# Projecting the last segment inside attention unit 0, with new step patterns for the other units

## The chip, the cores and the metric

The kernel runs on one core of a Trainium2 chip. The metric is the device time of one execution in microseconds, and lower is better. The time before is 1859.91 us, the median of three runs (1858.72, 1859.91 and 1860.71). A difference of about 0.2% (3.7 us) is the least that a measurement of this kernel can tell from no change.

## The reference

One transformer block on 2048 tokens of width 576 is computed in float32: adaptive layer norm, an attention with 32 heads of width 18 that works on four segments of 512 tokens and carries a memory from one segment to the next, its output projection, a second layer norm, and a gated feed-forward part with 4608 hidden columns.

```python
h = _layernorm(x) * (1 + ca) + sa
q, k, v = h @ wq, h @ wk, h @ wv            # 32 heads of 18 columns, N = 4 segments of L = 512 tokens
for s in range(N):
    logits = qs @ ks.T * scale + mask       # mask inside the segment
    a_dot  = softmax(logits) @ vs
    a_mem  = (phi(qs) @ M) / (phi(qs) @ z + 1e-6)
    o      = g * a_mem + (1 - g) * a_dot
    M, z   = M + phi(ks).T @ vs, z + phi(ks).sum(0)
x = x + ga * (o @ wo)
h = _layernorm(x) * (1 + cb) + sb
x = x + gb * ((silu(h @ w_gate) * (h @ w_up)) @ w_down)
```

phi(t) is t + 1 where t is positive and exp(t) elsewhere. ca, sa, ga and the rest come from one small product, silu(c) @ w_mod.

## The kernel before

Matrix products keep float32 accuracy by splitting each operand into a rounded high part and a low part, so one product takes three passes. A **projection tile** is 128 of the 1152 columns of k and q for one segment: 14 matmuls of 512 columns into one PSUM bank (the PSUM buffer `pp`, line 100), then two ScalarE copies out of it (`fh` rounded, `f` full, lines 513 and 514), a VectorE subtraction (`fl`, line 515), and stores to DRAM on SyncE's queue (`kD`, `qD`, and for the q columns phi(q) in `qF`, lines 519 to 532). A segment has nine tiles; tiles 0 to 4 hold k, 4 to 8 hold q.

**Phase 1** runs a loop over the four segments. For each it does the nine tiles (`proj`), for segments 0 to 2 also the v projection (`vproj`) and the memory (`mem`), and it prepares the next segment: `load_x`, the layer norm, and `trans_in` (transposes, `pt`, line 255), which leaves the activations as `hh`, `hl` and `hr`. Between these pieces stand two side jobs in small steps: `early` (scores for the row maxima of units 0 and 1) and `late_mod` (the remaining columns of w_mod; its last result is `gbB`, PSUM `pc`, line 371). In phase 1 a scheduler sets the order of instructions on each engine. Its SBUF pools are released at its end, the weights `wqkh` and `wqkl` among them.

**Phase 2** opens its own pools (`sk2`, `vp`, `wk2`, `op2` and others, and PSUM `ps2`) and walks over 33 **units**; units 0 to 31 are four heads of one segment each, eight units to a segment. In phase 2 the order of instructions is the order of the code. Unit u has 12 **score steps** (`a` in the patterns). A step does the score matmuls of one bank for unit u's exponentials (`p2_step`, line 656, then ScalarE's exponential, line 662) and those of one bank for unit u+2's row maxima (`p1_step`, line 184, then VectorE's masked maximum, line 199). The matmuls of the two kinds sit on different halves of the array's rows and are issued in turn. Three banks serve each kind.

The other events of a unit are letters of a pattern, a row of eleven slots in `PAT`: `V` multiplies the previous unit's exponentials with v (line 679), `E` copies the result out of PSUM on ScalarE (line 691, `avs`), `c` and `d` transpose and normalize it, `m` transposes the row maxima of unit u+1 and `n` copies them out on ScalarE (line 218, `mr`) and sends them by two DMAs (line 173) into the stacked operand `qs`, from which unit u+1's scores read them. `M` and `X` are a quarter of an extra product and its way out: in units 0 to 7 the v projection of segment 3 (`v_m`, line 803), from unit 9 on the output projection (`wo_m`, line 784). `P`, `Q`, `q`, `Y` prepare wo; `f` and `h` load phi(q); `A`, `B`, `C`, `D`, `G` compute the memory part; `R`, `S`, `T`, `Z`, `z` transpose the attention output; `l`, `p`, `x` do the second layer norm. Rows 0 and 1 of `PAT` serve even and odd units in the first half of a segment, rows 2 and 3 in the second half. `KP` says at which slot further transposes of the later units are issued. All of the events that use the PSUM tag `x` share two banks.

At the start of unit u, `load_unit(u + 3)` puts four loads on SyncE's queue (line 168, `ks<-kD` and `qs<-qD`); the row maxima of that unit begin one unit later. Unit 0 in the kernel before uses row 0 of `PAT`; `V`, `E`, `m`, `c` and `d` do nothing in it.

After unit 32 come the rest of the output projection and the feed-forward part, in which nothing is changed.

Of the kernel before, what the change touches and what calls it, by code (L numbers as in the profile page):

```python
# [15 lines left out]
P = 128  # L16
# [28 lines left out]
PM = ()  # L45
KP = (10, 8, 10, 8)
WW = (11, 15, 18, 22, 27)
# [12 lines left out]
E2 = 2  # L60
PAT = (("a a", "a D G V0123 m", "n", "E a", "a Q a M0 M1", "M2 a a M3", "c q X Y P d", "a", "h a a Z R z S T", "a f", ""),
# [3 lines left out]
LNA = 1  # L65
# [9 lines left out]
def block(ctx: ExitStack, tc: tile.TileContext, x, wqk, wv, wo, beta, wgu, wd, c, w_mod, wm01, out):  # L75
# [12 lines left out]
    def run(g):  # L88
        for _ in g:
            pass  # L90

    def mm14(ps, wh, wl, xh, xl, xr):
        k = 0
        for kt in range(5):
            if kt < 4:
                pairs = [(wh(kt), xh(kt)), (wl(kt), xh(kt)), (wh(kt), xl(kt))]
            else:
                pairs = [(wh(4), xr()), (wl(4), xr())]
            for a, b in pairs:
                nc.tensor.matmul(ps, lhsT=a, rhs=b, start=(k == 0), stop=(k == 13))  # L100
                k += 1

# [162 lines left out]

    p2, p2r, p7 = ExitStack(), ExitStack(), ExitStack()
    yx2 = pool(p7, "yx2", side="right")
# [5 lines left out]
    def v_ops(s, i, h):  # L273
# [6 lines left out]
        return ops + [(hr[:, tk], wvh[:, 4, sl]), (hr[:, tk], wvl[:, 4, sl])]  # L280

    with ExitStack() as p1:
        wq1 = pool(p1, "wq1")
        raw = pool(p1, "raw1", 2)
# [26 lines left out]

        wqkh = wq1.tile([P, 9, 5, P], F32R, tag="wqkh", name="wqkh")
        wqkl = wq1.tile([P, 9, 5, P], F32R, tag="wqkl", name="wqkl")
        bdm = w1.tile([P, 5, 8, VW], F32, tag="bdm", name="bdm")
# [190 lines left out]
        def proj(s, t):  # L505
            hh, hl, hr = hT[s]
            pp = ps.tile([P, L], F32, tag="p", name="pp", bufs=3)
            mm14(pp, lambda k: wqkh[:, t, k, :], lambda k: wqkl[:, t, k, :], lambda k: hh[k],
                 lambda k: hl[k], lambda: hr)
# [6 lines left out]
            k0, k1 = 128 * t, min(128 * t + 128, D)  # L516
            if k0 < D:
                n = k1 - k0
                nc.sync.dma_start(kD[s][k0:k1, 0:2, :], f32(fh[:n]).unsqueeze(1).to_broadcast([n, 2, L]))
                nc.sync.dma_start(kD[s][k0:k1, 2, :], f32(fl[:n]))  # L520
            q0, q1 = max(128 * t - D, 0), 128 * t + 128 - D
            if q1 > 0:
                n = q1 - q0
                r = P - n
                nc.sync.dma_start(qD[s][q0:q1, 0:3:2, :], f32(fh[r:]).unsqueeze(1).to_broadcast([n, 2, L]))
                nc.sync.dma_start(qD[s][q0:q1, 1, :], f32(fl[r:]))
                if s > 0:
                    e = pb.tile([P, L], F32, tag="pq1", name="pq1")
                    nc.vector.tensor_scalar(e[r:], f[r:], 0.0, None, op0=ALU.min)
                    nc.scalar.activation(e[r:], e[r:], AF.Exp)  # L530
                    nc.vector.scalar_tensor_tensor(e[r:], f[r:], 0.0, e[r:], op0=ALU.max, op1=ALU.add)
                    nc.sync.dma_start(qF[s][q0:q1, :], e[r:])
            return f
# [36 lines left out]

        for s in range(NSEG):
            gens = []
            if s == 0:
                gens.append(load_wv())
            if s + 1 < NSEG:
                gens.append(prep(s + 1))
            g = chain(*gens)
# [6 lines left out]
            for t in QKORD:  # L584
# [16 lines left out]
                if s > 1 or s == 1 and t > 4:  # L601
                    next(gl, None)
            tg = trans_in(s + 1) if s + 1 < NSEG else iter(())
            for i in range(4):
                if i == 3:
                    for _ in g:
                        pass
                if s < 3:
                    vproj(s, i)
# [9 lines left out]
            if s < 3:  # L619
                for _ in mem(s):  # L620
                    next(tg, None)
            for _ in tg:
# [7 lines left out]
    wk = pool(p2, "wk2", 2)  # L630
    opl_ = pool(p2, "op2")
    ps = pool(p2, "ps2", 2, space=PSUM)
# [92 lines left out]

    w3 = pool(p2r, "w3", side="right")
    o3 = pool(p2r, "o3", 2, side="right")
    yt = {}

    def yh(k, kb):  # L730
        return yt[1][:, k - 1, kb] if k else yt[0][kb]

    woh = w3.tile([P, 5, D], F32R, tag="woh", name="woh")
    wol = w3.tile([P, 5, D], F32R, tag="wol", name="wol")

# [50 lines left out]
    def wo_x(s, i, h):  # L786
# [3 lines left out]
        if h == 1:  # L790
            (nc.scalar if (s, i) == (2, 3) else nc.sync).dma_start(xD[s][:, i, :], xr)

    vst3 = {}
# [114 lines left out]
    def event(ev, u):  # L908
        n, a = ev[0], ev[1:]
        s, q = divmod(u, 8)  # L910
        if n == "V":
            for j in a:
# [11 lines left out]
        elif n == "d":  # L924
            comb_b(u - 1)
        elif n == "f" and s < 3 and q < 4:
            phi_q(s + 1, q + 1)
        elif n == "h" and s < 3 and q == 0:
            phi_q(s + 1, 0)
# [17 lines left out]
        elif n in "MX":  # L947
            w = u - 9
            if u < 8:
                if n == "M":  # L950
# [484 lines left out]
    with tc.manual_schedule():  # L1435
        new_stack(3, sk2)
        load_unit(3)
        for j in range(4):
            load_v(0, j)
        ot[0] = opl_.tile([P, 4, D], F32, tag="o0", name="o0")  # L1440
        for u in range(NU + 1):
            s, q = divmod(u, 8)
            if u:
                load_unit(u + 3)
            ma, mb = [], []
# [290 lines left out]
```

## Time and profile before

| | |
|---|---|
| median of three runs | 1859.91 us |
| profiled execution: its time / its span | 1856.97 us / 1855.2 us |
| TensorE busy in the span | 1816.8 us (98%), granted clock 0.996 |
| VectorE / ScalarE / GpSimd busy | 1492.6 / 958.2 / 495.8 us |
| segment 3's tiles start in the trace at | 191.4 us |
| unit 0 / unit 1 start in the trace at | 223.0 / 238.6 us |
| unit 32's product with v starts at | 566.2 us |

How to read it: the profiled execution took 1.8 us more than its span, and 2.9 us less than the median. TensorE's busy time counts a matmul from its issue to its end, and these overlap, so 98% does not mean that no time is lost: where the order makes TensorE wait a little, its records only grow longer. What a stage costs is better read from where it starts and where the next one starts. All times below are microseconds from the start of the span.

### The profile page before, as it was taken

What the parts mean: (1) busy time and instruction counts of PE and PEld (TensorE: products, weight loads), DVE (VectorE), ACT (ScalarE), POOL (GpSimd) and SP (SyncE); (2) the same over time, 40 slices, a digit from 0 to 9 for tenths busy, and PEclk for the clock granted to TensorE, in tenths of its full rate; (3) what the DMA queues carried; (4) which work ended last, traced back from release to release, by engine and by line L of the source; (5) the groups of instructions that cost most, each with busy time, mean ns of one, the idle gap of its engine ahead of it and who ended that gap; (6) DMA issues with size and microseconds to landing.
All of it is one profiled execution on the core that took longest, in us unless ns stands there. A gap on an engine that the chain in (4) does not pass through costs nothing.

```text
span 1855.2 us, 31128 instructions
## 1 busy us (share of the span) xinstructions
PE 1816.8 (98%) x11061; PEld 1518.0 (82%) x11061; DVE 1492.6 (80%) x3309; ACT 958.2 (52%) x2137; POOL 495.8 (27%) x702
## 2 busy tenths in 40 slices
PE   8999989999999999999999999999999999999999
PEld 5888756666667888888888888888888888888888
DVE  7566468888886888888888888758888888888887
ACT  6344457667776545445445444434454544544441
POOL 2010036454563345545544544300000000000000
PEclk9999999999999999999999999999999999999999
DMA  8677565558658654555555444395332333334331
GB/s 298 224 242 253 212 175 154 152 149 217 177 149 278 218 185 157 172 194 176 166 183 168 132 137 167 125 297 172 127 105 85 120 105 107 100 102 127 104 100 52
DMA packets 178562, 304.49 MB, mean 164 GB/s; under 512 B 25304, under 2 KB 108184, under 8 KB 176616
## 3 DMA queue, kind: packets, MB, share of 16 engines
q1 hardware_dynamic: 151032, 248.66, 42.7%
q10 hardware_dynamic: 27376, 53.86, 8.2%
q8 instruction: 87, 1.43, 0.3%
q14 instruction: 67, 0.55, 0.1%
HBM read 188.42 MB, written 113.33 MB: 163 GB/s over the span
## 4 chain that ended last, share of the span: by engine, by line
PE 87%; DVE 6%; DMA 4%; issue 1%; ACT 1%; SPq 1%; POOL 0%; ACTq 0%; DVEq 0%; POOLq 0%
PE A L1273 24%; PE pd L1401 13%; PE C L1273 12%; PE pd L1382 10%; PE B L1273 6%; PE pp L100 5%; PE av L679 3%; PE pw L784 3%; PE pv L545 2%; DVE junk L199 2%; PE s L184 2%; PE s L656 2%; DMA qs<-qD 1%; PE pn L862 1%; DMA y<-yD 1%
## 5 line engine op out<-in xcount | busy, mean ns | idle before, releaser
L1273 PE MATMUL A<-y,wh 128*128 128x512 f32 x1152 | 406.1, 393 | 1.1 <-ACT B L1319 0.7
L199 DVE CUSTOM_DVE_ANT_0 junk<-s,tri 128x384 bf16<-128x384 f32 (+3 forms) x512 | 222.0, 486 | 45.8 <-PE s L184 27.2
L1238 DVE TENSOR_TENSOR wl<-O,wh 128x256 fp32r<-128x256 f32 x504 | 253.7, 509 | 2.1 <-ACT wh L1237 1.6
L1273 PEld LDWEIGHTS A<-y,wh 128*128 128x128 f32 x1152 | 216.6, 188 | 45.9 <-ACT B L1319 2.2
L1273 PE MATMUL A<-y,wl 128*128 128x512 f32 x576 | 226.8, 394 | 0.0
L1387 DVE TENSOR_TENSOR acc<-acc,pd 128x576 f32<-128x576 f32 x216 | 162.3, 752 | 59.4 <-PE pd L1382 51.5
L1273 PE MATMUL C<-y,wh 128*128 128x512 f32 x576 | 202.9, 393 | 1.1 <-DVE cu L1296 1.1
L662 ACT ACTIVATE Pt<-s 128x512 f32<-128x512 f32 (+2 forms) x384 | 179.1, 525 | 44.7 <-PE s L184 24.4
L1237 ACT CAST wh<-O 128x256 fp32r<-128x256 f32 x504 | 197.5, 405 | 1.7 <-DMA yD<-st 0.8
L1401 PE MATMUL pd<-dh,ah 128*128 128x288 f32 x640 | 188.9, 295 | 0.5 <-DVE x L1405 0.5
L1401 PE MATMUL pd<-dh,al 128*128 128x288 f32 x640 | 189.0, 295 | 0.0
L1401 PE MATMUL pd<-dl,ah 128*128 128x288 f32 x640 | 188.7, 295 | 0.0
L1411 DVE TENSOR_TENSOR acc<-acc,pd 128x576 f32<-128x576 f32 x156 | 117.0, 750 | 87.9 <-PE pd L1401 87.2
L1228 POOL TENSOR_TENSOR O<-O 128x384 f32<-128x384 f32 x132 | 149.6, 1148 | 135.3 <-DMA O<-in_wgu_dram 61.5
L1342 ACT CAST ah<-sg 128x512 fp32r<-128x512 f32 x192 | 119.1, 621 | 77.2 <-DVE sg L1297 70.3
L1343 DVE TENSOR_TENSOR al<-sg,ah 128x512 fp32r<-128x512 f32 x192 | 136.3, 710 | 10.0 <-ACT ah L1342 9.9
L1382 PE MATMUL pd<-dh,ah 128*128 128x288 f32 x448 | 133.0, 297 | 0.0
L1382 PE MATMUL pd<-dh,al 128*128 128x288 f32 x448 | 132.5, 296 | 0.0
L1382 PE MATMUL pd<-dl,ah 128*128 128x288 f32 x448 | 132.3, 295 | 0.0
L184 PE MATMUL s<-ks,qs 54*128 54x512 f32 (+1 forms) x480 | 122.9, 360 | 8.2 <-DVE mx L199 4.2
L656 PE MATMUL s<-qs,ks 56*128 56x256 f32 (+3 forms) x512 | 124.5, 356 | 3.4 <-ACT Pt L662 2.8
L1401 PEld LDWEIGHTS pd<-dh,ah 128*128 128x128 f32 x640 | 120.7, 189 | 6.8 <-DVE x L1405 0.8
(388 smaller groups left out, 4337.2 us busy)
## 6 DMA issues: line engine op xcount, KB each, us to landing
O<-in_wgu_dram SPq DMA_DIRECT2D x36, 768.0 KB
O<-oD SPq DMA_DIRECT2D x36, 512.0 KB
oD<-O ACTq DMA_DIRECT2D x34, 512.0 KB
ks<-kD SPq DMA_DIRECT2D x64, 216.0 KB
qs<-qD SPq DMA_DIRECT2D x64, 216.0 KB
O<-in_wgu_dram SPq DMA_DIRECT2D x36, 384.0 KB
rD<-wr ACTq DMA_DIRECT2D x36, 336.0 KB
wr<-rD SPq DMA_DIRECT2D x35, 336.0 KB
```

Source lines behind the costliest of these rows:

```text
L184: nc.tensor.matmul(bank[:, n * o:n * o + n], lhsT=qst[b][r, h // 2, 128 * i:128 * i + 128], rhs=kst[b][r, h // 2, 0:n], start=True, stop=True)
L199: nc.vector.tensor_tensor_reduce(junk[:, :n], bank[:, n * o:n * o + n], tri[:, L - n:], 1.0, -3e38, op0=ALU.add, op1=ALU.max, accum_out=mx ...
L656: nc.tensor.matmul(bank[:, n * o:n * o + n], lhsT=kst[u % NB][r, g // 2, 128 * j:128 * j + 128], rhs=qst[u % NB][r, g // 2, 128 * j:L], st ...
L662: nc.scalar.activation(pt[:, hs[0]:hs[-1] + 1:2, :n], bank[:, :n * per].rearrange("p (a b) -> p a b", a=per), AF.Exp, scale=SCALE)
L1228: eng.tensor_tensor(o[:, d], o[:, a], o[:, b], op=op)
L1237: nc.scalar.copy(wh, o)
L1238: later.append(lambda: nc.vector.tensor_tensor(wl, o, f32(wh), op=ALU.subtract))
L1273: nc.tensor.matmul(bank, lhsT=a, rhs=b, start=(first and n == 0), stop=(n == 6), skip_group_check=not first)
L1343: later.append(lambda: nc.vector.tensor_tensor(al, src, f32(ah), op=ALU.subtract))
L1382: nc.tensor.matmul(pd[:, i, :288], lhsT=a[:, tk], rhs=w, start=(k == 0), stop=(k == 2))
L1387: nc.vector.tensor_tensor(o, o, pd[:, :, :288], op=ALU.add)
L1401: nc.tensor.matmul(pd[:, i, :288], lhsT=a[:, tk], rhs=w, start=(k == 0), stop=(k == 5))
```

## The change

The loop of phase 1 runs over segments 0 to 2 only, still transposes segment 3's activations at its end, and takes `late_mod` in more steps during segment 2, so that it ends there. The weights of the k and q projections lie in a pool of their own (`p2q`) that stays open. The pools of phase 2 are opened next, and unit 3's operands are loaded. Unit 0 then has a pattern row of its own, the fifth. In it `Wt` is a quarter of segment 3's projection tile t (`seg3`; three or four matmuls, with the PSUM bank from the shared tag `x`), and `W9` a quarter of the v projection that unit 0 had before. What follows a tile's last matmul is done in the three quarters after it: the copies, the VectorE part, the exponential for phi(q), the stores. The tiles' SBUF buffers are two sets cut out of `pq` and `vq`, which are free until then. At unit 1 the weights' pool is closed, and the pools for wo and for the attention output are opened in its place. The first two `phi_q` loads move from unit 0 to unit 1. Rows 0 to 3 of `PAT`, and `KP`, have other entries; no event is added to or taken from a unit by this.

```diff
-KP = (10, 8, 10, 8)
+KP = (9, 7, 10, 9)
-PAT = (("a a", "a D G V0123 m", "n", "E a", "a Q a M0 M1", "M2 a a M3", "c q X Y P d", "a", "h a a Z R z S T", "a f", ""),
+PAT = (("a a Q D", "a G V0123 m E q", "", "a a", "a M0 M1", "n a a c Y M2 d M3 X", "", "a a", "h f a R P Z S T", "", "z a"),
...
+       ("W0 W0 W0 W0 a a a", "W1 W1 W1 W1 W2 W2 W2 W2 a a a", "W3 W3 W3 W3 W4 W4 W4 W4", "a a a", "W5 W5 W5 W5 W6 W6 W6 W6", "a a a", "W7 W7 W7 W7", "W8 W8 W8 W8", "W9 W9", "W9 W9", "P"))
...
-        for s in range(NSEG):
+        for s in range(3):
...
-                if t < 5 and s < 3:
+                if t < 5:
                     pend = (t, f)
...
+                if s > 1 and t < 5:
+                    next(gl, None)
...
+    def seg3(t):
+        if not tmp3:
+            a = sk2.tile([P, 5, L], F32, tag="pq", name="tmpa").rearrange("p a b -> p (a b)")
+            b = vp.tile([P, 4, VC], F32, tag="vq", name="tmpb").rearrange("p a b -> p (a b)")
+            for v in (a, b):
+                tmp3.append([v[:, L * i:L * i + L] for i in range(4)])
+        f, fh, fl, e = tmp3[t % 2]
+        fh, fl = fh.bitcast(F32R), fl.bitcast(F32R)
+        pp = ps.tile([P, L], F32, tag="x", name="pp", bufs=XB)
+        ops = p_ops(3, t)
+        for c in range(WC):
+            for n in range(14 * c // WC, 14 * (c + 1) // WC):
+                nc.tensor.matmul(pp, lhsT=ops[n][0], rhs=ops[n][1], start=(n == 0), stop=(n == 13))
+            if c < 3:
+                yield
+        nc.scalar.copy(fh, pp)
+        nc.scalar.copy(f, pp)
+        yield
+        _, q1, r = q_rows(t)
+        nc.vector.tensor_tensor(fl, f, f32(fh), op=ALU.subtract)
+        if q1 > 0:
+            nc.vector.tensor_scalar(e[r:], f[r:], 0.0, None, op0=ALU.min)
+        yield
+        if q1 > 0:
+            nc.scalar.activation(e[r:], e[r:], AF.Exp)
+            nc.vector.scalar_tensor_tensor(e[r:], f[r:], 0.0, e[r:], op0=ALU.max, op1=ALU.add)
+        yield
+        k_store(3, t, fh, fl)
+        q_store(3, t, fh, fl)
...
+            if u == 1:
+                while s3q:
+                    seg3_step(-1)
+                p2q.close()
...
-                for ev in PAT[q // 4 * 2 + u % 2][k].split():
+                for ev in PAT[q // 4 * 2 + u % 2 if u else 4][k].split():
...
+                elif u == 0 and 2 <= k < 6:
+                    load_v(0, k - 2)
```

The first place is TensorE between the last segment's projection and unit 0. `pp` is a projection tile, `s` a bank of scores. Before, the last tile of segment 3 ends and the score steps of unit 0 follow one on another:

```order
L100 MATMUL pp<-hl_2191,wqkh 128x512
L100 MATMUL pp<-hr,wqkh 128x512
L100 MATMUL pp<-hr,wqkl 128x512
L656 MATMUL s_2602<-qs_982,ks_983 128x512
L184 MATMUL s_2605<-ks_991,qs_990 128x512
L184 MATMUL s_2612<-ks_991,qs_990 128x512
L656 MATMUL s_2611<-qs_982,ks_983 128x512
L656 MATMUL s_2618<-qs_982,ks_983 128x512
L184 MATMUL s_2619<-ks_991,qs_990 128x512
L184 MATMUL s_2626<-ks_991,qs_990 128x512
L656 MATMUL s_2625<-qs_982,ks_983 128x512
L656 MATMUL s_2634<-qs_982,ks_983 128x384
```

Now they begin behind the first tile of segment 3, three steps at a time, and the next tile follows:

```order
L807 MATMUL pp<-hl_2197,wqkh 128x512
L807 MATMUL pp<-hr,wqkh 128x512
L807 MATMUL pp<-hr,wqkl 128x512
L661 MATMUL s_2369<-qs_982,ks_983 128x512
L174 MATMUL s_2372<-ks_991,qs_990 128x512
L174 MATMUL s_2379<-ks_991,qs_990 128x512
L661 MATMUL s_2378<-qs_982,ks_983 128x512
L661 MATMUL s_2385<-qs_982,ks_983 128x512
L174 MATMUL s_2386<-ks_991,qs_990 128x512
L807 MATMUL pp<-hh_2190,wqkh 128x512
L807 MATMUL pp<-hh_2190,wqkl 128x512
L807 MATMUL pp<-hl_2194,wqkh 128x512
```

All nine tiles stand so between four groups of three steps; in each tile the matmuls that read `hr` come last.

The second place is SyncE's queue at the same point. `ks_2588` and `qs_2587` are unit 3's operands, `ks_983` and `qs_982` unit 0's buffers, which unit 4 takes over. Before, unit 3's loads stand behind all of segment 3's stores:

```order
L525 DMA qD_90<-fh 128x2x512
L526 DMA qD_90<-fl 128x512
L532 DMA qF_98<-pq_2547 128x512
L125 DMA ks_2588<-ones 10x8x128
L125 DMA ks_2588<-ones 2x8x128
L168 DMA ks_2588<-kD_91 54x2x512
L168 DMA qs_2587<-qD_87 54x2x512
```

Now unit 3's loads stand ahead of the first of these stores, and behind the last of them come the loads for unit 4:

```order
L297 DMA qD_90<-tmpa 128x2x512
L298 DMA qD_90<-tmpa 128x512
L826 DMA qF_98<-tmpa 128x512
L1033 DMA woraw<-in_wo_dram 128x576
L158 DMA ks_983<-kD_91 54x2x512
L158 DMA qs_982<-qD_87 54x2x512
```

So what waits for the end of the last tile on this queue is no longer unit 3's load but unit 4's.

The third place is ScalarE in unit 2, an even unit in the first half of a segment (row 0). `Pt` is a score bank's exponential, `mr` the copy of the row maxima, `avs` the copy of the product with v. Before:

```order
L662 ACTIVATE Pt<-s_2937 128x512
L218 COPY mr<-pmt 32x128
L691 COPY avs<-av 128x512
L662 ACTIVATE Pt<-s_2970 128x512
L662 ACTIVATE Pt<-s_2979 128x384
L662 ACTIVATE Pt<-s_2986 128x384
L662 ACTIVATE Pt<-s_3007 128x384
```

Now:

```order
L667 ACTIVATE Pt<-s_2907 128x512
L696 COPY avs<-av 128x512
L667 ACTIVATE Pt<-s_2936 128x512
L667 ACTIVATE Pt<-s_2945 128x384
L667 ACTIVATE Pt<-s_2952 128x384
L208 COPY mr<-pmt 32x128
L667 ACTIVATE Pt<-s_2974 128x384
```

The copy of the row maxima has moved behind the copy of the product with v and behind three exponentials.

More of the change, by code (lines that the diff above doesn't have):

```diff
@@ L90, in run @@
             pass
[L92 to L101, printed above, removed]
     cst = pool(ctx, "cst")
@@ L505, in proj @@
         def proj(s, t):
-            hh, hl, hr = hT[s]
             pp = ps.tile([P, L], F32, tag="p", name="pp", bufs=3)
-            mm14(pp, lambda k: wqkh[:, t, k, :], lambda k: wqkl[:, t, k, :], lambda k: hh[k],
-                 lambda k: hl[k], lambda: hr)
+            for n, (a, b) in enumerate(p_ops(s, t)):
+                nc.tensor.matmul(pp, lhsT=a, rhs=b, start=(n == 0), stop=(n == 13))
             f = pb.tile([P, L], F32, tag="pf", name="pf")
@@ L515, in proj @@
             nc.vector.tensor_tensor(fl, f, f32(fh), op=ALU.subtract)
[L516 to L521, printed above, removed]
+            k_store(s, t, fh, fl)
+            q_store(s, t, fh, fl)
+            q0, q1, r = q_rows(t)
             if q1 > 0:
[L523 to L526, printed above, removed]
                 if s > 0:
@@ L618, in block @@
             next(tg, None)
-            if s < 3:
-                for _ in mem(s):
-                    next(tg, None)
+            for _ in mem(s):
+                next(tg, None)
             for _ in tg:
@@ L1444, in block @@
                 load_unit(u + 3)
+            if u == 1:
+                while s3q:
+                    seg3_step(-1)
+                p2q.close()
+                w3 = pool(p2r, "w3", side="right")
+                o3 = pool(p2r, "o3", 2, side="right")
+                opl_ = pool(p2, "op2", side="right")
+                woh = w3.tile([P, 5, D], F32R, tag="woh", name="woh")
+                wol = w3.tile([P, 5, D], F32R, tag="wol", name="wol")
+                ot[0] = opl_.tile([P, 4, D], F32, tag="o0", name="o0")
             ma, mb = [], []
```

80 lines of the change are left out of this document (59 added, 21 removed), and 6 rows, old and new, of the table PAT.

## The prediction

> **What bounds the kernel now.** I read the change first, and then only the stretch that it touches: from segment 3's first projection tile, at 191.4 us, to the end of the units, at about 570 us. The page says how long the profiled execution was, and the windows view cuts the start of that stretch into segment 3's tiles, unit 0, unit 1 and unit 2. Columns: stretch, length, then busy time and instructions of TensorE, weight loads, VectorE, ScalarE and GpSimd, then the granted TensorE clock, the DMA share and GB/s.
>
> ```profile
> span 1855.2 us, 31128 instructions
> ...
> 191.40:223.00 31.60, 31.60 (x143) 25.08 (x141) 11.91 (x21) 14.60 (x26) 1.43 (x2) 1.00 0.61 213
> 223.00:238.60 15.60, 9.89 (x48) 6.53 (x47) 8.74 (x36) 8.20 (x17) 3.72 (x10) 0.72 0.74 207
> 238.60:251.00 12.40, 12.10 (x86) 6.89 (x87) 6.88 (x31) 6.74 (x16) 3.49 (x7) 0.81 0.66 207
> 251.00:262.00 11.00, 9.99 (x89) 6.19 (x92) 9.72 (x42) 6.99 (x16) 4.33 (x11) 1.00 0.49 141
> ```
>
> The first row is TensorE alone: busy all of 31.6 us, with VectorE at 11.9 and ScalarE at 14.6. The second is the opposite: unit 0 takes 15.6 us with TensorE busy for 9.9, at a clock of 0.72, and the clock is still 0.81 in unit 1. The chain of waits says what holds it.
>
> ```profile
> 193.51 15.40 PE pp L100 x66
> ...
> 211.13 11.90 PE pp L100 x51
> ...
> 225.23 0.60 DVE junk L199
> 225.84 0.60 DVE junk L199
> ...
> 230.46 8.05 DMA qs<-qD
> ...
> 238.65 0.89 PE s L184 x2
> ...
> 285.00 8.04 DMA qs<-qD
> ```
>
> Tiles go at 15.40 / 66 = 0.233 us a matmul. Unit 0 then ends on unit 3's operands: their last load is issued at 230.46 and lands 8.05 us later, and unit 1's first scores start at 238.65. In the queue this load stands behind the stores of all nine tiles. So unit 0 costs 15.6 us for little TensorE work, because a load came late and nothing else was left to do.
>
> The units behind it are another regime. The product with v happens once a unit, so its rows are their beat:
>
> ```profile
> 239.77 4.14 PE L679 MATMUL av<-Pt,vq 128*32 128x512 f32 x32
> 251.62 2.36 PE L679 MATMUL av<-Pt,vq 128*32 128x512 f32 x32
> 261.94 2.36 PE L679 MATMUL av<-Pt,vq 128*32 128x512 f32 x32
> 271.99 2.36 PE L679 MATMUL av<-Pt,vq 128*32 128x512 f32 x32
> ...
> 559.27 2.36 PE L679 MATMUL av<-Pt,vq 128*32 128x512 f32 x32 [0.30 <-POOL Pt L666]
> ```
>
> From unit 2 to unit 31 are 29 units in 307.65 us, 10.61 each. The view of waits between 251 and 566 us gives what TensorE and its weight loads waited for around the scores (total, times, longest):
>
> ```profile
> PEld s L184 <- DVE mx L199: 11.2, 36, 1.0
> PEld s L656 <- ACT Pt L662: 7.6, 24, 0.9
> PE s L656 <- ACT Pt L662: 2.5, 8, 0.5
> PE s L184 <- DVE mx L199: 2.2, 5, 0.9
> ```
>
> That is 23.5 us in all, many small waits for a score bank, and this is what other step patterns can act on.
>
> **Term 1: unit 0 inside the tiles.** Before, the two first windows are 31.6 + 15.6 = 47.2 us. Now the same TensorE work stands in one run. The tiles and what stood between them stay at 31.6 us (gbB's two matmul pairs and the transposes move ahead of the tiles, and cost the same there). To it come unit 0's extra product and its twelve score steps, at full clock. The product is 14 matmuls of 288 columns; for the steps I take those of unit 10, from each group's first score to the next operation behind it:
>
> ```profile
> 570.16 2.07 PE pw L784 x14
> ...
> 337.72 0.50 PE L184 MATMUL s<-ks,qs 54*128 54x512 f32 x1
> ...
> 338.51 0.40 PE L784 MATMUL pw<-woh,hh 128*128 128x288 f32 x1
> ...
> 340.04 0.44 PE L656 MATMUL s<-qs,ks 56*128 56x384 f32 x1
> ...
> 340.58 0.40 PE L784 MATMUL pw<-wol,hh 128*128 128x288 f32 x1
> ...
> 341.75 0.38 PE L656 MATMUL s<-qs,ks 56*128 56x256 f32 x1
> ...
> 342.59 0.66 PE L758 MATMUL pto<-ident,o 128*128 128x128 f32 x4
> ```
>
> Three steps in 0.79 us, two in 0.54, three narrow ones in 0.84: 0.27 us a step, 3.3 us for twelve. With the product's 2.1 us this makes 31.6 + 3.3 + 2.1 = 37.0 us.
>
> One wait is added. Tile 0 now stands alone at the front and ends with `hr`, where before the scheduler mixed tiles 0 and 1.
>
> ```profile
> 192.42 0.78 ACT L262 ACTIVATE hh<-pt,colv 128x512 fp32r<-128x512 f32 x1 [2.90 <-PE pt L255]
> ...
> 195.23 0.69 DVE L264 TENSOR_TENSOR hr<-hf,hr 64x512 fp32r<-64x512 f32 x1 [0.63 <-ACT hf L263]
> ```
>
> `hr` was ready at 195.9, 4.5 us after the tiles began; tile 0's twelve matmuls ahead of it take 2.8. So up to 1.7 us is lost, and nothing if `hr` comes earlier by the 2.90 us that ScalarE sat idle for transposes, which now stand ahead of the last memory matmuls. I take 0.8, the middle. The stretch becomes 37.8 us, a gain of 47.2 - 37.8 = **9.4 us**.
>
> The other engines have room in it: ScalarE's 14.6 + 8.2 = 22.8 us and VectorE's 11.9 + 8.7 = 20.6 us fit under 37.8. Each score step puts about 0.6 us on both, three steps at once, and at least one tile (14 x 0.233 = 3.3 us) stands behind each group, so their banks come free under it.
>
> **Term 2: the clock.** Unit 1 took 251.62 - 239.77 = 11.85 us, unit 2 10.32 and unit 3 10.05; unit 1's product with v alone took 4.14 us instead of 2.36. Without the idle stretch before it I expect unit 1 to take what unit 2 took: **1.5 us** gained (0 if TensorE still idles enough, 1.8 by unit 3).
>
> **Term 3: what is late next.** The load that held unit 1 is now 40 us early. Behind the last store, though, stand the four loads for unit 4, which unit 2 needs. How long a last tile takes to its last store, and four such loads to be issued:
>
> ```profile
> 222.62 0.40 PE L100 MATMUL pp<-hr,wqkl 128*128 128x512 f32 x1
> ...
> 227.08 0.32 SPq L532 DMA_DIRECT2D qF<-pq  x1
> ...
> 229.22 0.42 SPq L168 DMA_DIRECT2D ks<-kD  x1
> ...
> 230.46 0.34 SPq L168 DMA_DIRECT2D qs<-qD  x1
> ```
>
> From the tile's end at 223.0 to its store's issue were 4.1 us, 2.9 without the two VectorE maxima of 0.60 that stood between. Unit 1 starts 2.1 us after the tile, behind the extra product. So the loads begin 0.8 to 2.0 us into unit 1, the last is issued 1.2 us later, and with 8.05 us it lands 10.1 to 11.3 us into a unit of 10.3. The wait is 0 to 1.0 us; I take **0.6 us** lost. The Trainium skill ("DMA: Bandwidth & Descriptors", section "Anatomy of one DMA") has about 2.0 us fixed and bytes over 436 GB/s: an estimate of 4 us for these 864 KB, no wait, and a sum 0.6 us better. The 8.05 and 8.04 us of the chain speak against it here, and I go by them.
>
> **Term 4: the patterns of units 1 to 31.** Each unit keeps its events. Row 1 had four score steps in a row with nothing of TensorE between them, for three banks; now there are three, and part of the extra product behind. In row 0 `c` and `d` now stand among score steps. No row of before prices this. Two units with row 0 or 1 and like work differ by 10.32 - 10.05 = 0.27 us; over 31 units that is 8.4 us, which I take as the end on both sides. Since the listed waits total 23.5 us and the one clear edit (row 1, eight units) goes against them, I take a tenth of them: **2.0 us** gained.
>
> **Sum.** 9.4 + 1.5 - 0.6 + 2.0 = 12.3 us. The profiled execution took 1856.97 us, so 1844.7 on its scale; it lies 2.9 us under the median, so I forecast 1859.91 - 12.3 = **1847.6 us**. With the ends of term 4 and the small ones the likeliest case spans 1840 to 1857.
>
> **Rivals.**
>
> *The row maxima arrive late (slower).* In row 0, ScalarE's copy `mr` now stands behind `avs` and three exponentials; behind it wait two DMAs on SyncE's queue, and the next unit's first score on TensorE.
>
> ```profile
> 337.83 0.26 ACT L218 COPY mr<-pmt 32x128 f32<-32x128 f32 x1 [1.77 <-PE pmt L214]
> 337.99 0.57 ACT L691 COPY avs<-av 128x512 f32<-128x512 f32 x1
> ...
> 338.47 1.33 ACT L662 ACTIVATE Pt<-s 128x512 f32<-128x512 f32 x3
> ...
> 338.11 1.29 SPq L173 DMA_DIRECT2D qs<-mr  x2
> ...
> 344.78 0.47 PE L656 MATMUL s<-qs,ks 56*128 56x512 f32 x1
> ```
>
> The DMAs were issued by 339.40 and read at 344.78 without a wait, so they land within 5.4 us. The copy comes 0.57 + 1.33 and a little, some 2.2 us, later. From a landing of 3.2 us on, each of the seven units with row 0 waits; at 5.4 it is 2.2 x 7 = 15.4 us. Without term 4's gain that ends at 1859.91 - 10.3 + 15.4 = 1865. It beats the whole gain from about 4.7 us on. For it speaks only that no row shows the landing of such a small transfer, against it that no unit shows a wait for one. By the fixed 2.0 us of the Trainium skill ("DMA: Bandwidth & Descriptors", the same section) it would cost nothing. Chance 0.07.
>
> *The patterns lose.* At 0.3 us a unit 31 units lose 9.3 us, and 10.3 - 9.3 leaves 1 us: 1859, no change. The units' spread allows it. Chance 0.10.
>
> *The patterns win.* If half of the 23.5 us goes, the gain is 10.3 + 11.7 = 22 us: 1838. Chance 0.12.
>
> *The tiles don't cover the steps.* Tiles use two PSUM banks instead of three, and their copies queue behind exponentials. If each of the four groups of steps holds the next tile for 1.5 us, 6 us of term 1 go: 1853.6. Against it stands the 3.3 us tile that hides them. Chance 0.08.
>
> **How the numbers follow.** The likeliest case keeps 0.63. The range goes from 1838 (the patterns win) to 1857 (the bad end of term 4); beyond it lie the slower rival and most of the no-change one, under 0.2. Taking 0.2%, 3.7 us, as what a measurement can tell: faster 0.83 (the likeliest, the winning patterns and the uncovered tiles), within it 0.10, slower 0.07.
>
> **What would show it.** Right: a stretch of about 38 us from the first tile to unit 1, TensorE busy throughout at a clock of 1.00; unit 1's product with v at 2.36 us; no wait of unit 1 on `qs<-qD`, and at most 1 us of unit 2. Wrong: waits of tile matmuls on ScalarE or on stores inside unit 0, a clock below 0.9 in unit 1, waits on `qs<-mr`, or products with v that follow each other by clearly more than 10.61 us on average.

## The result and the profile after

The changed kernel takes 1849.26 us (median of four runs, 1847.35 to 1852.14) against 1860.06 for the kernel before beside it (four runs, 1858.72 to 1860.71): a ratio of 0.9946, 95% interval 0.9932 to 0.9959, or about 10 us less (7.6 to 12.6 by the interval). The same kernel, run again later, gave 0.9947 (0.9935 to 0.9959). The forecast was 1847.6 us.

The profiled execution of the changed kernel took 1849.43 us. Its windows view, cut at the matching places (tiles and unit 0; unit 1; the start of unit 2; unit 3), has the columns of the prediction's first fence:

```profile
span 1847.4 us, 31122 instructions
...
193.59:228.50 34.91, 34.91 (x174) 27.68 (x174) 18.13 (x49) 16.43 (x33) 4.75 (x10) 1.00 0.67 221
228.50:242.90 14.40, 10.15 (x85) 6.30 (x84) 10.21 (x39) 8.44 (x20) 5.07 (x11) 0.92 0.86 250
242.90:254.00 11.10, 10.61 (x83) 6.32 (x83) 6.60 (x24) 6.03 (x14) 1.37 (x4) 0.80 0.46 140
254.00:264.00 10.00, 10.00 (x89) 6.27 (x89) 7.94 (x43) 7.04 (x18) 3.90 (x10) 1.00 0.54 166
```

The 15.6 us in which TensorE was busy for 9.9 are gone from unit 0: tiles and score steps together take 34.9 us, with TensorE busy for all of it. But the second row looks like the old unit 0. Unit 1 lasts 14.4 us with TensorE busy for 10.15, and behind it the clock is 0.80. The chain of waits names what ended it, at the same stretch where it named `qs<-qD` before:

```profile
226.67 1.84 PE pw L860 x14
228.51 0.43 PE s L661
...
234.53 8.20 DMA qs<-mr
242.87 0.76 PE s L661
```

Unit 1 starts at 228.51 (before: 238.65). Unit 2 starts at 242.87, when the row maxima land that were issued 8.20 us earlier. The timeline's rows of the product with v give the beat:

```profile
229.43 2.36 PE L684 MATMUL av<-Pt,vq 128*32 128x512 f32 x32 [0.25 <-issue]
244.54 3.73 PE L684 MATMUL av<-Pt,vq 128*32 128x512 f32 x32
255.40 2.36 PE L684 MATMUL av<-Pt,vq 128*32 128x512 f32 x32
...
539.09 2.36 PE L684 MATMUL av<-Pt,vq 128*32 128x512 f32 x32
550.54 4.32 PE L684 MATMUL av<-Pt,vq 128*32 128x512 f32 x32
559.33 1.71 PE L684 MATMUL av<-Pt,vq 128*32 128x512 f32 x16
```

From these rows and those of before the whole span divides into stages (us; "u" is the start of that unit's product with v):

| stage | before | after |
|---|---|---|
| start to segment 3's first tile | 191.45 | 193.59 |
| first tile to u1 | 48.32 | 35.84 |
| u1 to u2 | 11.85 | 15.11 |
| u2 to u3 | 10.32 | 10.86 |
| u3 to u30 | 287.81 | 283.69 |
| u30 to u32 | 16.45 | 20.24 |
| u32 to the end (unchanged code) | 1289.00 | 1288.07 |

Three things happened: 12.5 us came from the tiles and unit 0, of which 3.3 went again between u1 and u2; 4.1 us came from 27 units of new patterns; and 3.8 us were lost in the last two units. The tiles also start 2.1 us later. Some of that is work that stood between the tiles before (transposes and `gbB`) and now stands ahead of them, so not all of the 12.5 us is saved: u1 comes 10.3 us earlier. How much of the 2.1 us is chance can't be told: the other kernels with moved tiles start them from 193.2 to 195.9 us, and a kernel whose first phase is that of before starts them at 193.32. For the 27 units the windows view says the same in one row for each kernel, before first, then after:

```profile
262.00:550.00 288.00, 276.76 (x2451) 186.07 (x2454) 249.49 (x1051) 208.51 (x470) 156.31 (x332) 1.00 0.59 167
```

```profile
255.40:539.10 283.70, 276.72 (x2449) 185.71 (x2448) 248.40 (x1047) 207.06 (x470) 157.09 (x332) 1.00 0.61 170
```

TensorE's busy time is the same 276.7 us, at a clock of 1.00; its idle time fell from 11.2 to 7.0.

### The profile page after: what moved, and what is told of

The parts are those of the page before. It is cut to its first block, busy times and chain, and to the rows that moved or that the text cites. A ratio compares the mean times of both kernels' runs of the same rounds, so it can differ in the third digit from the quotient of the medians.

```text
span 1847.4 us, 31122 instructions
## 1 busy us (share of the span) xinstructions
PE 1816.2 (98%) x11061; PEld 1517.4 (82%) x11061; DVE 1490.4 (81%) x3309; ACT 955.5 (52%) x2137; POOL 495.3 (27%) x702
## 4 chain that ended last, share of the span: by engine, by line
PE 89%; DVE 5%; DMA 3%; ACT 1%; issue 1%; POOL 0%; SPq 0%; ACTq 0%; DVEq 0%
PE A L1335 24%; PE pd L1463 13%; PE C L1335 12%; PE pd L1444 10%; PE B L1335 6%; PE pp L523 4%; PE av L684 4%; PE s L661 2%; PE pv L552 2%; PE pw L784 2%; PE s L174 2%; PE pp L807 2%; DVE junk L189 1%; DMA qs<-mr 1%; PE pn L919 1%
## 5 line engine op out<-in xcount | busy, mean ns | idle before, releaser
L1300 DVE TENSOR_TENSOR wl<-O,wh 128x256 fp32r<-128x256 f32 x504 | 249.3, 500 | 2.1 <-ACT wh L1299 1.6
L1463 PEld LDWEIGHTS pd<-dl,ah 128*128 128x128 f32 x640 | 120.6, 188 | 7.1
```

The source lines that it names most:

```text
L1300: later.append(lambda: nc.vector.tensor_tensor(wl, o, f32(wh), op=ALU.subtract))
L1463: nc.tensor.matmul(pd[:, i, :288], lhsT=a[:, tk], rhs=w, start=(k == 0), stop=(k == 5))
```

## The experiments

Each edit is made to the changed kernel unless another is named. The kernel before was run beside each group of four: 1858.49 us beside "old patterns", "before, new patterns", "no interleaving" and "unit 4's load early"; 1858.15 beside the three with v and wo ahead and "old rows at the end"; 1859.36 beside "late load", "changed, again" and the two with the maxima on ScalarE's queue. The ratios and their intervals come from all runs of a kernel; the three middle columns come from one profile of each. "Start" below is from the first tile to u3, the sum of the stages in which the transfers matter.

| kernel | start | u3 to u30 | u30 to u32 | ratio, 95% |
|---|---|---|---|---|
| before | 70.49 | 287.81 | 16.45 | 1 |
| changed | 61.81 | 283.69 | 20.24 | 0.9946 (0.9932 to 0.9959) |
| changed, again | 62.38 | 283.42 | 18.90 | 0.9947 (0.9935 to 0.9959) |
| old patterns | 62.86 | 287.59 | 16.44 | 0.9970 (0.9958 to 0.9982) |
| before, new patterns | 70.52 | 282.51 | 20.42 | 0.9980 (0.9970 to 0.9989) |
| late load | 70.13 | 283.24 | 17.36 | 0.9982 (0.9973 to 0.9990) |
| no interleaving | 57.92 | 283.78 | 20.51 | 0.9940 (0.9926 to 0.9953) |
| unit 4's load early | 65.45 | 283.24 | 18.91 | 0.9963 (0.9950 to 0.9976) |
| v and wo ahead | 60.76 | 284.72 | 20.29 | 0.9953 (0.9941 to 0.9966) |
| same, unit 4 too | 58.42 | 286.00 | 17.35 | 0.9934 (0.9922 to 0.9947) |
| v and wo ahead, no interleaving | 60.17 | 283.31 | 17.33 | 0.9932 (0.9918 to 0.9946) |
| old rows at the end | 61.95 | 283.33 | 16.45 | 0.9955 (0.9943 to 0.9968) |
| maxima on ScalarE's queue | 62.35 | 286.54 | 20.52 | 0.9944 (0.9931 to 0.9957) |
| unit 4 too, maxima on ScalarE's queue | 61.02 | 283.52 | 18.89 | 0.9934 (0.9922 to 0.9946) |

**The two halves apart.** First the changed kernel with the patterns of before, then the kernel before with the new patterns.

```diff
-KP = (9, 7, 10, 9)
+KP = (10, 8, 10, 8)
...
-PAT = (("a a Q D", "a G V0123 m E q", "", "a a", "a M0 M1", "n a a c Y M2 d M3 X", "", "a a", "h f a R P Z S T", "", "z a"),
+PAT = (("a a", "a D G V0123 m", "n", "E a", "a Q a M0 M1", "M2 a a M3", "c q X Y P d", "a", "h a a Z R z S T", "a f", ""),
...
```

> The changed kernel with rows 0 to 3 of PAT and KP of the kernel before, and unit 0's own row kept. Theory A (the patterns give about 4 us in units 3 to 30, and unit 0 gives the rest): about 1853, and products with v that follow each other as before, 10.6 us on average from unit 3 to 30 instead of 10.5. Rival B (the patterns are worth nothing, the whole gain is unit 0's): 1849, the same as the changed kernel. Rival C (the new rows cost time and hide part of unit 0's gain): about 1845.

```diff
-KP = (10, 8, 10, 8)
+KP = (9, 7, 10, 9)
...
-PAT = (("a a", "a D G V0123 m", "n", "E a", "a Q a M0 M1", "M2 a a M3", "c q X Y P d", "a", "h a a Z R z S T", "a f", ""),
+PAT = (("a a Q D", "a G V0123 m E q", "", "a a", "a M0 M1", "n a a c Y M2 d M3 X", "", "a a", "h f a R P Z S T", "", "z a"),
...
```

> The kernel before with only the new rows 0 to 3 of PAT and the new KP; unit 0 uses the new row 0, and segment 3's tiles stay in phase 1. Theory A: 2 to 4 us faster than before, 1856 to 1858. Rival B: 1860, no change. Rival C: slower than before, 1863 or so. In all of them unit 1 still waits about 3 us on unit 3's load at the start.

They took 1854.2 and 1854.12 us. By the ratios the moved projection gains 5.6 us (3.3 to 7.8) and the patterns gain 3.7 (2.0 to 5.6); together 9.3, and the whole change measured 10.0. So the two halves add up, and Theory A held in both. The patterns are worth more than the 2.0 us forecast; the moved projection is worth little over half of the 10.3 us that terms 1 to 3 gave it.

**Which part of the move gains.** The move does two things to the start: the score steps stand between the tiles, and unit 3's loads stand ahead of the stores. One kernel has the second without the first, one the first without the second.

```diff
-       ("W0 W0 W0 W0 a a a", "W1 W1 W1 W1 W2 W2 W2 W2 a a a", "W3 W3 W3 W3 W4 W4 W4 W4", "a a a", "W5 W5 W5 W5 W6 W6 W6 W6", "a a a", "W7 W7 W7 W7", "W8 W8 W8 W8", "W9 W9", "W9 W9", "P"))
+       ("W0 W0 W0 W0 W1 W1 W1 W1 W2 W2 W2 W2", "W3 W3 W3 W3 W4 W4 W4 W4", "W5 W5 W5 W5 W6 W6 W6 W6", "W7 W7 W7 W7 W8 W8 W8 W8", "a a a", "a a a W9 W9", "W9 W9 a a a", "a a a", "", "", "P"))
```

> The changed kernel with unit 0's twelve score steps behind all nine tiles again, in four groups with the extra product between them; pools and unit 3's load stay early. Theory A (laying the steps under the tiles is what gains, since twelve steps in a row are bound by VectorE at about 0.6 us each plus the last tile's VectorE work): 4 to 7 us slower than the changed kernel, 1853 to 1856, of the 10 us that unit 0 gained. Rival (the early load alone makes the gain, and the place of the steps is worth nothing): 1849.

```diff
-        load_unit(3)
         for u in range(NU + 1):
             s, q = divmod(u, 8)
+            if u == 1:
+                load_unit(3)
             if u:
                 load_unit(u + 3)
```

> The changed kernel with one edit: unit 3's four loads are issued at the start of unit 1, behind segment 3's stores, as in the kernel before; the score steps stay between the tiles. Theory T (what holds units 1 and 2 are transfers queued behind segment 3's stores, and the gain is unit 3's load going ahead of them): the loads are issued at about 233 us and land some 8 us later, unit 1's first scores wait to about 241, its product with v starts near 242 instead of 229.4, unit 2's near 252 instead of 244.5, and the time is about 1857, no better than the kernel before. Rival I (interleaving the steps with the tiles is itself worth most of the 9.4 us): unit 1 starts by 232 and the time stays near 1849 to 1851.

Without interleaving the kernel is no slower than the changed one, against Theory A: 1847.17 us. Its products with v show why:

```profile
232.91 2.36 PE L684 MATMUL av<-Pt,vq 128*32 128x512 f32 x32
242.62 2.36 PE L684 MATMUL av<-Pt,vq 128*32 128x512 f32 x32
252.10 2.36 PE L684 MATMUL av<-Pt,vq 128*32 128x512 f32 x32
```

Unit 1 comes 3.5 us later than in the changed kernel, but unit 2 comes 1.9 us earlier and unit 3 3.3 earlier, all at full clock; between 222 and 256 us TensorE waits for no transfer. With the late load the time is 1856.68, as Theory T had it, and the views of waits and chain show the wait of the kernel before again:

```profile
PE s L174 <- DMA qs<-qD: 12.6, 1, 12.6
...
233.66 7.36 DMA qs<-qD
```

TensorE finishes the tiles and steps at 228.5 as planned and then waits 12.6 us for unit 3's load. The starts make a square: neither part 70.5 us (the kernel before with the new patterns), interleaving alone 70.1, the early load alone 57.9, both 61.8. (The kernel with neither also has its v loads and buffers as before, so that corner is not a single edit away.) The early load is the gain. Interleaving alone brings nothing. On top of the early load it costs 3.9 us at the start in these profiles, because it brings unit 1 forward and unit 2 must then wait for a transfer; in the times the two orders are not apart, their intervals overlap.

**What holds unit 2.** The first attempt moved unit 4's loads ahead of the last tile.

```diff
-            if u:
+            if u > 1:
                 load_unit(u + 3)
...
+                if u == 0 and k == 7:
+                    load_unit(4)
```

> The changed kernel with unit 4's four loads put on SyncE's queue in unit 0, behind tile 7's stores and ahead of tile 8's, instead of at unit 1's start. Theory A (unit 2's late start comes of these loads being issued late, and the transfer of the row maxima being queued behind them): no wait of 3.2 us before unit 2, no clock below 1.00 in units 1 and 2, unit 2's product with v at 2.36 us; 3.2 us and 1.4 us less, about 1844.5. Rival (the transfers are slow because of the stores' volume, not the loads' place): the wait on the row maxima stays, about 1849.

It took 1852.77 us, with a start 3.6 us longer than the changed kernel's, which neither theory had. The view of waits from 185 to 262 us:

```profile
POOL woraw L1037 <- DMA woraw<-in_wo_dram: 17.5, 1, 17.5
ACT woh L1039 <- POOL woraw L1037: 6.2, 1, 6.2
PE s L661 <- ACT Pt L667: 5.9, 1, 5.9
```

Now `woraw`, the load of wo, stands behind unit 4's loads and the last stores. GpSimd waits for it, ScalarE's rounding of it waits for GpSimd, ScalarE's exponentials are queued behind, and TensorE waits 5.9 us. A wait was exchanged for a longer one. The next three kernels took the loads of v and wo out of the crowd: wo's first piece (`P`) to the front of unit 0 and the four loads of v behind unit 3's; then also unit 4's loads ahead of the last tile; then the first of these without interleaving.

```diff
-       ("W0 W0 W0 W0 a a a", "W1 W1 W1 W1 W2 W2 W2 W2 a a a", "W3 W3 W3 W3 W4 W4 W4 W4", "a a a", "W5 W5 W5 W5 W6 W6 W6 W6", "a a a", "W7 W7 W7 W7", "W8 W8 W8 W8", "W9 W9", "W9 W9", "P"))
+       ("P W0 W0 W0 W0 a a a", "W1 W1 W1 W1 W2 W2 W2 W2 a a a", "W3 W3 W3 W3 W4 W4 W4 W4", "a a a", "W5 W5 W5 W5 W6 W6 W6 W6", "a a a", "W7 W7 W7 W7", "W8 W8 W8 W8", "W9 W9", "W9 W9", ""))
...
         load_unit(3)
+        for j in range(4):
+            load_v(0, j)
...
-                elif u == 0 and 2 <= k < 6:
-                    load_v(0, k - 2)
```

> The changed kernel with the first wo load (288 KB) and the four v loads (1.25 MB) put on SyncE's queue ahead of segment 3's tiles instead of among and behind them. Theory D (unit 2 starts late because the DMA engines are full from 225 to 235 us, so that whatever is issued behind the last stores takes 8 us; 1.5 MB less there are some 4 us at 355 GB/s): GpSimd no longer waits about 12 us on woraw, the wait before unit 2 falls from 3.2 us to under 1, its product with v is back at 2.36 us, and the time is 1844 to 1846. Rival (only the order on the queue counts, and unit 4's loads still stand behind the last stores): the wait stays at 3 us, 1849.

> As the run before it, and unit 4's loads ahead of tile 8's stores as well. Theory D: no wait before unit 2 at all, 1843 to 1845; what made that place of unit 4's loads slow by itself was GpSimd waiting on woraw behind them. Rival: the loads hold up tile 8's stores and the row maxima behind them, as before, and it is slower than without, 1850.

> Unit 0's twelve score steps behind all nine tiles, with the wo load and the v loads ahead of the tiles. Theory D (laying steps under tiles brings unit 1 forward by 3.5 us, and only the late transfers took that away): 2 to 4 us slower than the same loads with the steps under the tiles. Rival (the end of the stores sets unit 2's start in either order): the same time as with the steps under the tiles.

The first took 1849.67 us, no better than the changed kernel: its chain still has `qs<-mr`, for 7.58 us, and unit 2 still waits 3.0 us for it. So the outcome that its rival gave came, and 1.5 MB less in the crowd did not help. The second took 1846.75 and the third 1846.29; both are faster than the kernel before, and their medians are 2 to 3 us better than the changed kernel's, but the intervals of the ratios overlap. Theory D had the third slower than the first by 2 to 4 us, and it was faster by 3.4, of which units 30 to 32 alone make 3.0 in the profiles (17.33 against 20.29). At the start the two are level (60.17 and 60.76), but the third's unit 1 ran at a clock of 0.50 from 233 to 239 us, so these two do not say what the order of the steps is worth. In the second, unit 2 is nearly free and the wait, which Theory D had gone, moves one unit on. Chain, in two places, and TensorE's timeline:

```profile
232.89 6.15 DMA qs<-mr
...
244.85 6.79 DMA qs<-mr
```

```profile
239.17 0.46 PE L661 MATMUL s<-qs,ks 56*128 56x512 f32 x1 [0.66 <-DMA qs<-mr]
...
251.77 0.46 PE L661 MATMUL s<-qs,ks 56*128 56x512 f32 x1 [3.18 <-DMA qs<-mr]
```

So the row maxima are late again and again while SyncE's queue holds larger transfers. They are two transfers of 8 KB each by the view of DMA issues; the expectation below has them at 4 KB. Two kernels sent those of units 2 and 3 over ScalarE's queue, the first from the changed kernel, the second from the one with unit 4's loads ahead.

```diff
-            nc.sync.dma_start(f32(qst[b][64 * e + 54:64 * e + 56]).rearrange("p a t -> p (a t)"), mr[16 * e:16 * e + 16])
+            (nc.scalar if u in (2, 3) else nc.sync).dma_start(f32(qst[b][64 * e + 54:64 * e + 56]).rearrange("p a t -> p (a t)"), mr[16 * e:16 * e + 16])
```

> The changed kernel with one edit: the two 4 KB transfers that carry the row maxima of units 2 and 3 are issued by ScalarE on its own queue, not on SyncE's. Theory F (what is late in unit 2 is everything queued on SyncE's queue behind tile 8's stores and unit 4's loads, each in turn): the maxima land within 4 us of their issue and the wait on qs<-mr is gone, but unit 4's loads still land at about 241 to 242, and TensorE waits at the first row-maximum matmul of unit 2 for them instead; product with v of unit 2 at 243.5 to 244.5, time 1848 to 1849.5. Rival M (the maxima alone were late): unit 2's product with v starts near 240.5, unit 3's near 251, time about 1845.

> The kernel with unit 4's loads ahead of the last tile's stores and the early loads of v and wo, with one more edit: the row maxima of units 2 and 3 go over ScalarE's queue. Theory F: in that kernel unit 4's loads are in time, and only the maxima, queued on SyncE's queue, held unit 3 (3.2 us at 248.6) and a little of unit 2 (0.6 us); on a queue of their own they land within 4 us, both waits go, unit 3's product with v starts near 249.5 instead of 252.9, at 2.36 us instead of 3.71, and the time is 1842 to 1844. Rival S (the DMA engines are saturated whatever the queue): the maxima still take 6 us, unit 3 still waits about 3 us, time 1846.5.

Theory F failed in both. The waits of TensorE on `qs<-mr` are gone in both, but u2 comes 15.4 us after u1 in the first (15.1 in the changed kernel) and 14.0 in the second (10.3 in its base), and the times are 1851.17 and 1847.44. The windows from 235 to 245 us show it for the second, base first and then the edit:

```profile
235.00:245.00 10.00, 9.34 (x87) 6.08 (x85) 8.71 (x38) 7.29 (x17) 3.74 (x12) 1.00 0.58 191
```

```profile
235.00:245.00 10.00, 9.38 (x46) 5.88 (x50) 6.84 (x31) 6.94 (x16) 4.29 (x10) 0.61 0.57 193
```

TensorE is as busy in both, but does 46 matmuls instead of 87, at a clock of 0.61. The chain of the edited kernel has ScalarE's own issue ahead of it:

```profile
232.43 1.28 ACTq L163
...
233.75 0.64 ACTq L163
...
234.43 0.59 ACT avs L696
```

The two issues hold ScalarE for 1.9 us, and the copy `avs` and the exponentials come later. TensorE waits 1.11 us for one of them at 235.57, its longest wait there; it is busy for 0.9 of the 2 us from 234, and from 238 to 247 the clock is 0.50.

Nor did the maxima land much sooner. ScalarE's queue carried nothing else then, and the view of DMA queues in steps of 0.1 us shows its last packets at 241.4 us in the first kernel and 238.3 in the second: 8.0 and 5.9 us after the first issue (233.36 and 232.43), against 8.20 and 6.15 us on SyncE's queue in their bases. So their place in SyncE's queue can't alone be what makes them late. In these kernels they take 6 to 8 us on either queue while the large transfers are under way; this part of Rival S held. For unit 3 in the second kernel, with a DMA share of 0.04, they took 2.2 us (250.07 to 252.3).

**The last two units.** The rows of before for units 30 on, to see whether u30 to u32 can be had back; and the changed kernel once more.

```diff
-                for ev in PAT[q // 4 * 2 + u % 2 if u else 4][k].split():
+                for ev in (PAT_OLD if u >= 30 else PAT)[q // 4 * 2 + u % 2 if u else 4][k].split():
```

> The changed kernel with the old rows of PAT for units 30, 31 and 32 alone. Theory E (the new rows leave TensorE idle in units 30 and 31, where no more row maxima are taken, so that the clock falls to 0.82 there): the clock stays at 1.00, unit 31's product with v takes 2.36 us instead of 4.3, and 3 to 4 us are gained, about 1845.5. Rival (the lower clock there is chance): 1849.

> The changed kernel itself once more. Theory X (the slow clock at units 30 to 32, a granted clock near 0.8 and a product with v of 4.32 us in unit 31, comes with an execution and not with the order): units 30 to 32 take about 17.4 us, as in the two kernels with the early loads of v and wo, or about 20.2 as in the first profile, one or the other. Rival O (it belongs to this order, whose units reach this point at the same phase each time): 20.2 us again. Time 1847 to 1851 either way.

With the old rows the two units take 16.45 us at a clock of 1.00, as Theory E had it and as in all three profiles with old rows there; but the time was 1850.26, no better. The changed kernel again took 18.9 us there, neither of Theory X's two values, but not Rival O's 20.2 either. With the new rows they take 17.3 us in three profiles, 18.9 in three and 20.2 to 20.5 in five. Where they take more than 17.4, unit 31's product with v is slow, as in these rows of the changed kernel again (3.08 us; 4.32 in its first profile) beside the kernel with v and wo ahead and no interleaving:

```profile
541.68 2.36 PE L684 MATMUL av<-Pt,vq 128*32 128x512 f32 x32
553.04 3.08 PE L684 MATMUL av<-Pt,vq 128*32 128x512 f32 x32
560.58 1.71 PE L684 MATMUL av<-Pt,vq 128*32 128x512 f32 x16
```

```profile
539.06 2.36 PE L684 MATMUL av<-Pt,vq 128*32 128x512 f32 x32
549.57 2.36 PE L684 MATMUL av<-Pt,vq 128*32 128x512 f32 x32
556.39 1.71 PE L684 MATMUL av<-Pt,vq 128*32 128x512 f32 x16
```

So the new order costs 0.9 us there, and up to 4.1 with a slow clock that some profiles have and others of the same rows have not. What triggers it stays open. That its removal didn't show in the time is not explained either; the stage behind, in which nothing is changed, varies from 1287.0 to 1291.9 us between profiles, and the changed kernel's own two profiles took 1849.43 and 1854.16 us. A 3 us effect in one profile is at the edge of what these runs can show.

## Why the prediction was right, and where it was not

The total was forecast at 12.3 us less and measured at about 10, inside the range and on the right side. That it came so near is in part luck: timed apart, terms 1 to 3 gave 5.6 us instead of 10.3, and term 4 gave 3.7 instead of 2.0. By its terms:

- **Term 1 (9.4 us).** The stretch from the first tile to unit 1 took 34.9 us instead of the 37.8 forecast, and as the tiles start 2.1 us later, unit 1's first scores come 10.1 us earlier (238.65 to 228.51). TensorE was busy throughout at 1.00, and no `hr` wait appeared; the 0.8 us for it was not needed. The reading of the profile, that unit 0 was long because a load came late, was right. The credit was wrong: the term was worked out as TensorE work laid end to end, and the late-load kernel shows that this alone gives nothing. The moved load is what gains. The term also stopped at the start of unit 1, and unit 1 could not keep what it was given.
- **Term 2 (1.5 us) failed.** Unit 1's product with v did take 2.36 us, but unit 1 did not take unit 2's former 10.3 us: it took 15.1, and the slow clock moved one unit on, to unit 2, behind the new wait.
- **Term 3 (-0.6 us) was mis-sized**, and is the main error. From u1 to u3 take 25.97 us; at the two units of 10.3 us that terms 2 and 3 started from it would be 20.6, so 5.4 us are lost. The 8.05 us that the prediction took for the landing was about right: the maxima, issued right behind unit 4's loads, took 8.20. The shorter estimate from the Trainium skill ("DMA: Bandwidth & Descriptors", section "Anatomy of one DMA") was not: the page gives that fit for transfers that GpSimd issues, and these are SyncE's, with others under way. What failed was the step "the loads begin 0.8 to 2.0 us into unit 1". They began 4.4 us into it:

```profile
228.26 0.59 ACT L810 CAST tmpa<-pp 128x512 fp32r<-128x512 f32 x1 [1.88 <-DMA qD<-tmpa]
...
231.81 0.32 SPq L826 DMA_DIRECT2D qF<-tmpa  x1
232.18 0.67 SPq L1033 DMA_DIRECT2D woraw<-in_wo_dram  x1
232.94 0.34 SPq L158 DMA_DIRECT2D ks<-kD  x1
...
234.53 1.45 SPq L163 DMA_DIRECT2D qs<-mr  x2
```

  With two sets of SBUF buffers the last tile's copy waits 1.88 us for the stores of tile 6; the last store is issued 5.1 us after the tile's matmuls end (226.67), where 2.9 to 4.1 were forecast; wo's load goes in front; and behind unit 4's loads stand unit 2's row maxima, which the term did not list among what is queued there. The prediction named waits on stores as a sign that it would be wrong, but gave them no price.
- **Term 4 (2.0 us) had the right sign and half the size.** Timed apart the patterns gain 3.7 us (2.0 to 5.6). The four listed waits, 23.5 us before, between the same times in the changed kernel:

```profile
PEld s L174 <- DVE mx L189: 11.4, 40, 0.9
...
PEld s L661 <- ACT Pt L667: 7.1, 32, 1.0
...
PE s L174 <- DVE mx L189: 1.3, 3, 0.6
...
PE s L661 <- ACT Pt L667: 0.7, 2, 0.4
```

  make 20.5 us, 3.0 less. The loss in units 30 to 32 was not foreseen.
- **The rivals.** The slower one, row maxima late in row 0 of the pattern, did not come: between 251 and 566 us TensorE waits 0.8 us for `qs<-mr`, once. A wait for the same transfer did appear, but in the one place where the queue is full, not seven times. That tiles would not cover the steps is refuted by the first window's length, 34.91 us where 37.8 were forecast. The patterns neither lost nor won big.
- **The range.** It was added up a little short: with term 4 at its bad end (8.4 us lost instead of 2.0 gained) the sum gives 1858.0, not 1857, and a tenth of 23.5 us is 2.35, not 2.0. Nothing above hangs on either.

## What to carry to other kernels

When a load that is late is moved forward, list everything that is issued while the same stores are under way, the smallest transfers too and on whatever queue, with the time of each issue, and ask which of them the next stage reads first: here the wait moved to the next one in line. Before work is interleaved to fill a stall, ask whether the transfer that ended the stall moves as well; here moving the load gave all of the gain and the interleaving none. And a wait of some 3 us costs more than its length, since in these profiles the clock was slow behind it.

## What the runs showed of the hardware

In these runs a small transfer was as slow as the large ones under way with it, on their queue or another. The row maxima, 2 x 8 KB, took 8.20, 7.58, 6.15 and 6.79 us on SyncE's queue in four places, against 7.36 us for the end of a 216 KB load. On ScalarE's queue, which carried nothing else, they took 8.0 and 5.9 us beside the same large transfers, and 2.2 us at a DMA share of 0.04. The DMA share was 0.86 in unit 1 of the changed kernel.

Behind each of the four waits of TensorE for `qs<-mr` of 3.0 to 3.4 us its clock was 0.50. The windows of the changed kernel in steps of 2.5 us, for one of them:

```profile
238.50:241.00 2.50, 1.17 (x10) 0.78 (x8) 2.26 (x12) 1.43 (x5) 2.16 (x5) 0.91 0.96 202
241.00:243.50 2.50, 0.63 (x3) 0.66 (x5) 0.41 (x1) 0.00 (x0) 0.49 (x3) 0.50 0.85 174
243.50:246.00 2.50, 2.50 (x14) 0.79 (x14) 1.92 (x6) 1.64 (x3) 0.00 (x0) 0.50 0.68 222
```

The clock falls inside the wait (239.7 to 242.87) and is still 0.50 up to 246, with TensorE busy all the time. A wait of 0.66 us, in the kernel with unit 4's loads ahead, left it at 1.00. The Trainium skill ("TensorE: Matmul & The Clock Gate", the part on the HAM clock gate) has half clock after an idle window of about 3.4 us, and full clock again after about as long a busy one; the trace, half clock within a wait of 3.2 us and full clock again in the window after 248.5, agrees nearly.

But the clock also fell without such a wait, and stayed low longer. In the kernel with unit 4's loads ahead and the maxima on ScalarE's queue it fell behind a wait of 1.11 us and was 0.50 from 238 to 247 with TensorE busy for all 9 us. In the kernel with v and wo ahead and no interleaving it fell behind a stretch from 230 to 233 with TensorE busy for 1.76 of 3 us (longest wait 0.99 us); in the kernel with no interleaving alone, 2.05 of 3 us from 229 to 232 left it at 1.00. So that rule of the Trainium skill, taken as one wait of that length, does not describe these drops. No long wait stands ahead of the slow clock of units 30 to 32 in the changed kernel; the longest of TensorE from 538 to 551 us is 0.72 us:

```profile
548.40 1.06 PE L1095 MATMUL pt<-ident,yq 128*96 128x128 f32 x4 [0.72 <-PE pto L758]
```

Its windows there:

```profile
540.00:550.00 10.00, 8.81 (x71) 6.11 (x63) 4.95 (x12) 6.72 (x17) 7.54 (x13) 0.89 0.39 120
550.00:560.00 10.00, 10.00 (x74) 5.33 (x75) 2.14 (x7) 6.92 (x16) 4.98 (x8) 0.77 0.06 22
```

TensorE is busy for 8.81 of 10 us and then for all 10, and the clock is 0.89 and 0.77. In finer windows it is 0.50 from 548 to 554, behind 4 us (545 to 549) in which TensorE is busy for 2.86. In the kernel with v and wo ahead and no interleaving TensorE is busy for 2.90 of the same 4 us, and the clock stays at 1.00. So an order that leaves TensorE thinly used there runs at half clock in some profiles and not in others; no run here shows what decides it.

ScalarE is held while it issues transfers: the two of the row maxima took 1.28 and 0.64 us of it.
